# LayerNorm statistics of an out-projection, taken in halves between residual adds in a fixed VectorE order, and a last output tile finished in 128 columns

## The chip, the cores and the metric

One core of one Trainium2 chip. The metric is the device time of one execution in microseconds (us). All runs that are compared here are fast, with a granted TensorE clock of 0.999 or 1.0. A profile's span, from its first to its last instruction, is 1.7 to 2.1 us shorter than the time measured for the same execution. Ratios are the mean time of one kernel's fast runs over that of the other's of the same rounds, so they are not quite the ratio of the medians that are quoted.

## The reference, cut to what matters

Two attention blocks and two token MLPs alternate on `x` of 2048 rows and 1024 columns. The weights are the same both times.

```python
x = x + A(layernorm(x), wqkv, wo)      # local dilated attention, 32 heads, window 8, step 2
x = x + B(layernorm(x), w1, b1, w2, b2)# gelu MLP over the token axis, 3584 hidden
x = x + A(layernorm(x), wqkv, wo)
x = x + B(layernorm(x), w1, b1, w2, b2)
```

The change concerns two places. The first is the end of each `A`: the product with `wo` (the out-projection), the residual add and the statistics of the LayerNorm that follows. The second is the very last tile of the last `B`.

## The kernel before

The out-projection works on 16 tiles of 128 rows. A tile has two halves of 512 columns. Each half takes 8 matmuls into one of two buffers `m` in PSUM (the memory that matmuls write), and then a residual add on VectorE empties the buffer. The first four tiles are interleaved with the last two visits of the attention: a visit makes scores, an exponential on ScalarE, masks on VectorE (`mask`), the products with the values, two passes of a reciprocal on ScalarE, and a normalization on VectorE (`norm`). `chain_` fixes the order of what it wraps on one engine, and `in_order` does so for TensorE; everything else is placed by the scheduler.

```python
psm = pool("psm", 2, space=PSUM)                 # the two m buffers
...
def stats(x, mul, eps):                          # VectorE, then ScalarE
    s = st("bn", [P, NDC, 6])
    for cc in range(NDC):
        nc.vector.bn_stats(out=s[:, cc, :], in_=x[:, cc * 512:(cc + 1) * 512])
    mv = st("mv", [P, 2])
    nc.vector.bn_aggr(out=mv[:], in_=s[:])
    rs = st("rs", [P, 1])
    rsqrt(rs[:], mv[:, 1:2], mul, eps)           # two small ScalarE passes: Ln, Exp
    return mv[:, 0:1], rs
def norm_act(dst, x, mean, rs):
    bi = st("bi", [P, 1])
    nc.vector.tensor_scalar(out=bi[:], in0=mean, scalar1=rs[:], scalar2=-1.0, ...)
    nc.scalar.activation(out=dst, in_=x, func=ACT.Identity, bias=bi[:], scale=rs[:])
...
# out_proj: half(n) = 8 matmuls into an m buffer, add(n) = residual add of it, and
def ln():
    norm_act(h2[c][i][:], xn[:], *stats(xn, 1.0 + EPS, eps2))
...
for vis in range(2 * NU):                        # attention; the last two visits carry tiles 0..3
    ...
    chain_("DVE", mask, 0, 1)                    # (in the last two visits)
    ...
    chain_("DVE", norm.pop())
    for n in range(2):
        half, add, store, ln = out_proj(0, 2 * b + n, ...)
        in_order(half, 0)
        chain_("DVE", add, 0)
        if n == 0:
            chain_("DVE", mask, 2, 3)
        elif lns:
            lns.pop(0)()
        in_order(half, 1)
        chain_("DVE", add, 1)
        store()
        lns.append(ln)
...
for k, (c, i) in enumerate(order[4:]):           # tiles 4..15
    for n in range(2):
        half(n)
        add(n)
    store()
    lns.append(ln)
    for _ in range(2):
        if lns:
            lns.pop(0)()
...
# gemm2, one output tile: 28 matmuls of 512 columns for each half, an add, one store of the tile
for dc in range(NDC):
    for ft in range(FT):
        nc.tensor.matmul(aps[dc], lhsT=w2t[...], rhs=g[...][:, ..., dc * 512:(dc + 1) * 512], ...)
    nc.vector.scalar_tensor_tensor(out=xo[:, dc * 512:(dc + 1) * 512], in0=aps[dc], scalar=b2_sb[...],
                                   in1=xs[:, dc * 512:(dc + 1) * 512], op0=ALU.add, op1=ALU.add)
nc.sync.dma_start(out=dst, in_=xo[:])
```

The softmax here doesn't subtract the row's maximum and nothing guards it: scores larger than these inputs give would overflow.

## Time and profile before

Median 1297.89 us of three runs (1297.88 to 1298.09).

The page's first lines for the kernel before give busy time, share of the span and number of instructions of each engine.

```profile
span 1296.0 us, 19495 instructions
PE 1288.2 (99%) x8414; PEld 591.7 (46%) x8414; DVE 419.3 (32%) x851; ACT 373.4 (29%) x628; POOL 2.4 (0%) x15
```

TensorE (PE) is busy for 99% of the span, so a change to the work of VectorE (DVE) or ScalarE (ACT) can only pay where TensorE waits for it. The list of waits has one entry of the out-projection; its columns are who waited for whom, us in total, times, and the longest.

```profile
PE m L467 <- DVE xn L474: 1.1, 2, 0.6
```

This is the matmul into `m` waiting for the residual add that empties the buffer. The list shows only the two longest of these waits, because a matmul's recorded end lies 0.16 us after the next one could start (379 ns recorded, 216 ns from start to start), and shorter stalls hide inside that. The starts tell more. Measured between weight-load starts, the kernel before has four late matmuls in each out-projection:

| late by, ns | 1st | 2nd | 3rd | 4th | first to last weight load, us |
|---|---|---|---|---|---|
| layer 1 | 188 | 76 | 731 | 101 | 57.587 |
| layer 2 | 190 | 73 | 731 | 97 | 57.580 |

The timeline of layer 1 shows why. Its columns are start, duration, engine, line, operation, output and inputs, count, and in brackets the idle time before it and what ended it. PEld is TensorE's weight load.

```profile
209.28 1.00 DVE L398 TENSOR_TENSOR Pm<-pc,band 32x640 bf16<-32x640 bf16 x2
210.32 0.69 DVE L180 BATCH_NORM_STATS2 bn<-xn 128x6 f32<-128x512 bf16 x1
210.93 0.67 DVE L474 TENSOR_TENSOR xn<-m,xr 128x512 bf16<-128x512 f32 x1
...
211.66 1.39 PEld L467 LDWEIGHTS <-oT 128*128 128x128 bf16 x7 [0.30 <-issue]
...
213.42 1.24 ACT L193 ACTIVATE h<-xn,bi,rs 128x1024 bf16<-128x1024 bf16 x1 [0.28 <-DVE bi L192]
213.47 0.46 PE L383 MATMUL s<-qB,kT 128*32 128x160 bf16 x16
...
214.57 0.78 ACT L386 ACTIVATE pc<-s,shift 128x640 bf16<-128x640 f32 x1
...
216.52 0.69 DVE L437 TENSOR_TENSOR oT<-acc,rd 128x512 bf16<-128x512 f32 x1
217.13 0.68 DVE L474 TENSOR_TENSOR xn<-m,xr 128x512 bf16<-128x512 f32 x1
217.84 0.99 DVE L398 TENSOR_TENSOR Pm<-pc,band 32x640 bf16<-32x640 bf16 x2
217.87 1.60 PEld L467 LDWEIGHTS <-oT 128*128 128x128 bf16 x8 [0.20 <-issue]
218.86 0.21 DVE L192 TENSOR_SCALAR bi<-mv,rs 128x1 f32<-128x1 f32 x1
218.99 0.68 DVE L180 BATCH_NORM_STATS2 bn<-xn 128x6 f32<-128x512 bf16 x1
219.59 0.67 DVE L474 TENSOR_TENSOR xn<-m,xr 128x512 bf16<-128x512 f32 x1
...
220.32 1.89 PE L467 MATMUL m<-wo,oT 128*128 128x512 bf16 x8 [0.57 <-DVE xn L474]
```

The first stall ends at 211.66: the add at 210.93 stood behind half a tile's statistics (L180, 0.69 us). The second ends at 217.87, when the third tile's first add (217.13) has emptied its buffer. The third, the large one, ends at 220.32: the add at 219.59 stood behind two masks (L398), a bias multiply (L192) and another half of statistics (L180). The fourth, of 0.1 us, comes later than the lines shown: the fifth tile's first add (225.57) stood behind the normalization of the last visit. One detail mattered later: on ScalarE the `h` activation of the first tile (L193, 1.24 us) started at 213.42, just ahead of the scores of the next visit at 213.47, and the exponential of these scores (L386) could start only at 214.57.

The tail is the last 512-column add and the store behind it, here in the timeline of the kernel before and then in its list of transfers (size, us from issue to landing).

```profile
1292.24 0.75 DVE L556 SCALAR_TENSOR_TENSOR xo<-m,b_sb,xs 128x512 bf16<-128x512 f32 x1 [5.29 <-PE m L553]
1293.02 0.34 SPq L558 DMA_DIRECT2D out_dram<-xo  x1
```

```profile
out_dram<-xo SPq DMA_DIRECT2D x1, 256.0 KB, 2.0
```

### The profile page before, as it was taken

To read this page: it belongs to the slowest core of one execution; us is meant where nothing else is said; L and a number is where in the kernel's file an instruction comes from. 1 tells how busy PE (TensorE), PEld (TensorE's weight loads), DVE (VectorE), ACT (ScalarE), POOL (GpSimd) and SP (SyncE) were. 2 spreads that over 40 slices of the span, in tenths; PEclk is the share of its full clock that TensorE was granted. 3 is DMA by queue.
4 is the path that set the end of the run, shared out by engine and by line. 5 is a ranking of instruction groups with operands and counts; after the bars stand their busy time and mean duration, and the time that the engine had idled before them with its cause. 6 is when DMAs were issued, how large, how long until landed. Compare 5 with 4: busy or idle time off the path is not lost.

```text
span 1296.0 us, 19495 instructions
## 1 busy us (share of the span) xinstructions
PE 1288.2 (99%) x8414; PEld 591.7 (46%) x8414; DVE 419.3 (32%) x851; ACT 373.4 (29%) x628; POOL 2.4 (0%) x15
## 2 busy tenths in 40 slices
PE   9999999999999999999999999999999999999998
PEld 4444444444444444444444444444444444444443
DVE  7457778810000022322300667688000000111111
ACT  5456665531111110000023666654211111000000
POOL 0000000000000000000000000000000000000000
PEclk9999999999999999999999999999999999999999
DMA  8411123652222235465510111246423222334330
GB/s 235 82 45 47 51 82 115 208 145 82 65 82 75 57 108 140 130 160 135 130 32 1 48 49 50 80 150 211 122 65 91 73 60 84 98 106 140 113 92 33
DMA packets 201574, 125.54 MB, mean 97 GB/s; under 512 B 39824, under 2 KB 183184, under 8 KB 201488
## 3 DMA queue, kind: packets, MB, share of 16 engines
q1 hardware_dynamic: 201488, 124.30, 33.8%
q8 instruction: 66, 1.08, 0.4%
q14 instruction: 20, 0.16, 0.0%
HBM read 96.48 MB, written 16.78 MB: 87 GB/s over the span
## 4 chain that ended last, share of the span: by engine, by line
PE 97%; DVE 1%; ACT 1%; issue 0%; DMA 0%; SPq 0%; DVEq 0%
PE m L352 17%; PE s L553 15%; PE s L510 15%; PE m L553 7%; PE m L510 7%; PE acc L510 7%; PE acc L553 7%; PE m L467 7%; PE m L337 4%; PE m L255 4%; PE s L383 2%; PE acc L418 1%; PE acc L422 1%; DVE xn L474 0%; PE m L268 0%; DVE Pm L398 0%
## 5 line engine op out<-in xcount | busy, mean ns | idle before, releaser
L510 PEld LDWEIGHTS <-w 128*128 128x128 bf16 x1792 | 175.4, 98 | 211.4
L553 PEld LDWEIGHTS <-w 128*128 128x128 bf16 x1792 | 175.3, 98 | 211.5
L352 PE MATMUL m<-hT,wqk 128*128 128x512 bf16 x1024 | 231.7, 380 | 0.0
L510 PE MATMUL s<-h,w 128*128 128x512 bf16 x896 | 202.8, 379 | 0.0
L553 PE MATMUL s<-g,w 128*128 128x512 bf16 x896 | 199.9, 379 | 0.0
L556 DVE SCALAR_TENSOR_TENSOR xo<-s,b_sb,xs 128x512 bf16<-128x512 f32 x32 | 24.0, 751 | 540.7 <-PE s L553 538.6
L352 PEld LDWEIGHTS <-wqk 128*128 128x128 bf16 x1024 | 95.3, 98 | 117.9 <-issue 10.7
L398 DVE TENSOR_TENSOR Pm<-pc,band 32x640 bf16<-32x640 bf16 x256 | 123.6, 483 | 65.8 <-ACT pc L386 56.3
L467 PE MATMUL m<-wo,oT 128*128 128x512 bf16 x512 | 112.5, 379 | 1.2 <-DVE xn L474 1.1
L510 PE MATMUL acc<-h,w 128*128 128x512 bf16 x448 | 103.9, 379 | 0.0
L553 PE MATMUL acc<-g,w 128*128 128x512 bf16 x448 | 100.6, 379 | 0.0
L553 PE MATMUL m<-g,w 128*128 128x512 bf16 x448 | 99.3, 379 | 0.0
L510 PE MATMUL m<-h,w 128*128 128x512 bf16 x448 | 99.0, 379 | 0.0
L174 ACT ACTIVATE ln<-mv,eps 128x1 f32<-128x1 f32 x64 | 18.9, 295 | 233.3 <-DVE mv L182 227.6
L517 ACT ACTIVATE g<-s,b_sb 128x1024 bf16<-128x1024 f32 x28 | 31.2, 1114 | 166.9 <-PE s L510 166.9
L467 PEld LDWEIGHTS <-oT 128*128 128x128 bf16 x512 | 49.5, 98 | 62.6 <-issue 4.5
L363 DVE COPY qB<-qs 32x512 bf16<-32x512 bf16 x136 | 38.1, 280 | 90.4 <-ACT qs L359 89.1
L255 PE MATMUL m<-wv,hT 128*128 128x512 bf16 x256 | 56.1, 379 | 0.7 <-ACT hT L249 0.7
L337 PE MATMUL m<-wv,hT 128*128 128x512 bf16 x256 | 55.4, 379 | 0.0
L359 ACT CAST qs<-m 128x512 bf16<-128x512 f32 x64 | 37.5, 586 | 49.0 <-PE m L352 49.0
L386 ACT ACTIVATE pc<-s,shift 128x640 bf16<-128x640 f32 x64 | 51.2, 799 | 0.3 <-PE s L383 0.3
L356 ACT CAST kT<-m 128x512 bf16<-128x512 f32 x64 | 37.5, 586 | 46.4 <-PE m L352 46.4
(57 smaller groups left out, 674.7 us busy)
## 6 DMA issues: line engine op xcount, KB each, us to landing
w<-in_B_w_dram SPq DMA_DIRECT2D x56, 512.0 KB, 3.8
w<-in_B_w_dram SPq DMA_DIRECT2D x64, 448.0 KB, 4.6
wqk<-in_A_wqkv_dram SPq DMA_DIRECT2D x16, 512.0 KB, 4.8
xa<-xn SPq DMA_DIRECT2D x32, 256.0 KB, 2.3
xs<-xa SPq DMA_DIRECT2D x32, 256.0 KB, 3.2
wv<-in_A_wqkv_dram SPq DMA_DIRECT2D x8, 512.0 KB, 5.5
wo<-in_A_wo_dram SPq DMA_DIRECT2D x8, 512.0 KB, 5.5
xr<-in_A_x_dram SPq DMA_DIRECT2D x16, 256.0 KB, 3.3
```

The source lines that it names most:

```text
L255: r = nc.tensor.matmul(pss_[k, n][:], lhsT=hT[:, kt, cols(*order[k])], rhs=wv[n][kt // 4][:, kt % 4, :], start=(kt == 0), stop=(kt == KD - 1))
L337: nc.tensor.matmul(ps[:], lhsT=hT[:, kt, cols(c, i)], rhs=wv[n][kt // 4][:, kt % 4, :], start=(kt == 0), stop=(kt == KD - 1))
L352: mm = nc.tensor.matmul(ps[:], lhsT=wts[part][:, kt, (g % 2) * P:(g % 2 + 1) * P], rhs=hT[:, kt, lo:lo + 512], start=(kt == 0), stop=(kt = ...
L356: nc.scalar.copy(out=kT[u % 2][:, ls], in_=ps[:])
L359: nc.scalar.copy(out=qs[:], in_=ps[:])
L363: nc.vector.tensor_copy(out=qB[u % 2][hp, h, ls], in_=qs[hp, :])
L386: nc.scalar.activation(out=pc[:].rearrange("p (n t) h k -> p n (t h k)", n=2), in_=ss[:, :, 0:2 * HG * GW], func=ACT.Exp, scale=scale, bia ...
L398: mm = nc.vector.tensor_tensor(out=Pm[rp, :, s0:s0 + HB, r * KG:r * KG + GW].rearrange("p h t k -> p t h k"), in0=pc[rp], in1=mk, op=ALU.mult)
L467: mm = nc.tensor.matmul(ps[:], lhsT=oT[g][:, cols(c, i)], rhs=wo[n][g // 4][:, g % 4, :], start=(g == 0), stop=(g == NG - 1))
L510: nc.tensor.matmul(pairs[fl][0][dc], lhsT=wt[c][:, i, fl * P:(fl + 1) * P], rhs=h2[c][i][:, dc * 512:(dc + 1) * 512], start=(k == 0), stop ...
L517: nc.scalar.activation(out=g[fb][:, fl, :].rearrange("p (n d) -> p n d", n=2), in_=t[:], func=ACT.Gelu_apprx_tanh, bias=b1_sb[:, ft:ft + 1])
L553: nc.tensor.matmul(aps[dc], lhsT=w2t[ft // HF][:, ft % HF, c::DIL], rhs=g[ft // GF][:, ft % GF, dc * 512:(dc + 1) * 512], start=(ft == 0), ...
```

## The change

Its intent: VectorE does at most one half of a tile's statistics between two residual adds, in a fixed order, and computes a tile's bias one step after its statistics, so that it need not wait for ScalarE. The normalization of the last visit moves from ahead of the fifth tile's first add to behind it. The last output tile's second half is computed as 384 and 128 columns and stored in three pieces, so that less work is left after the last matmul.

```diff
-        def ln():
-            norm_act(h2[c][i][:], xn[:], *stats(xn, 1.0 + EPS, eps2))
+        def ln_a():
+            chain_("DVE", stat_half, 0)
+        def ln_b():
+            chain_("DVE", stat_half, 1)
+            chain_("DVE", aggregate)
+            t["rs"] = st("rs", [P, 1])
+            rsqrt(t["rs"][:], t["mv"][:, 1:2], 1.0 + EPS, eps2)
+        def ln_c():
+            chain_("DVE", bias)
+            nc.scalar.activation(out=h2[c][i][:], in_=xn[:], func=ACT.Identity, bias=t["bi"][:], scale=t["rs"][:])
...
+    def ln_step():
+        if late:
+            late.pop()()
+        if lns:
+            parts = lns[0]
+            parts.pop(0)()
+            if len(parts) == 1:
+                late.append(lns.pop(0)[0])
... last two visits:
-                elif lns:
-                    lns.pop(0)()
+                else:
+                    ln_step()
                 in_order(half, 1)
                 chain_("DVE", add, 1)
                 store()
-                lns.append(ln)
+                lns.append(list(ln))
+                if n:
+                    ln_step()
... ahead of tile 4:
-        chain_("DVE", norm.pop())
... tiles 4 to 15:
                 half(n)
-                add(n)
+                chain_("DVE", add, n)
+                ln_step()
+                if norm:
+                    chain_("DVE", norm.pop())
... last tile:
+        parts = [(0, 512, aps[0]), (512, 512, aps[1])]
+        final = not to_hT and (c, i) == order[-1]
+        if final:
+            parts[1:] = [(512, 384, aps[1][:, 0:384]), (896, 128, s_tile()[:, 0, 0:128])]
+        for lo, w, ap in parts:
             ... 28 matmuls of w columns, the add of w columns
+            if final:
+                nc.sync.dma_start(out=dst[:, lo:lo + w], in_=xo[:, lo:lo + w])
+        if not final:
+            nc.sync.dma_start(out=dst, in_=xo[:])
```

More of the change, by code (lines that the diff above doesn't have):

```diff
@@ L478, in store, with stat_half, aggregate, bias @@
             h2[c][i] = vhp.tile([P, D], BF16, name="h2", tag="vh")
-        def ln():
-            norm_act(h2[c][i][:], xn[:], *stats(xn, 1.0 + EPS, eps2))
-        return half, add, store, ln
+        t = {}
+        def stat_half(cc):
+            if cc == 0:
+                t["s"] = st("bn", [P, NDC, 6])
+            return nc.vector.bn_stats(out=t["s"][:, cc, :], in_=xn[:, cc * 512:(cc + 1) * 512])
+        def aggregate():
+            t["mv"] = st("mv", [P, 2])
+            return nc.vector.bn_aggr(out=t["mv"][:], in_=t["s"][:])
+        def bias():
+            t["bi"] = st("bi", [P, 1])
+            return nc.vector.tensor_scalar(out=t["bi"][:], in0=t["mv"][:, 0:1], scalar1=t["rs"][:], scalar2=-1.0, op0=ALU.mult,
+                                           op1=ALU.mult)
+        def ln_a():
[8 more added lines that the diff above has]
+            nc.scalar.activation(out=h2[c][i][:], in_=xn[:], func=ACT.Identity, bias=t["bi"][:], scale=t["rs"][:])
+        return half, add, store, (ln_a, ln_b, ln_c)
+    lns, late = [], []
+    def ln_step():
[6 more added lines that the diff above has]
+                late.append(lns.pop(0)[0])
     pss_ = {}
@@ L550, in gemm2 @@
         aps, _ = pair(i * DIL + c)
-        for dc in range(NDC):
+        parts = [(0, 512, aps[0]), (512, 512, aps[1])]
[3 more added lines that the diff above has]
+        for lo, w, ap in parts:
             for ft in range(FT):
-                nc.tensor.matmul(aps[dc], lhsT=w2t[ft // HF][:, ft % HF, c::DIL],
-                                 rhs=g[ft // GF][:, ft % GF, dc * 512:(dc + 1) * 512],
+                nc.tensor.matmul(ap, lhsT=w2t[ft // HF][:, ft % HF, c::DIL], rhs=g[ft // GF][:, ft % GF, lo:lo + w],
                                  start=(ft == 0), stop=(ft == FT - 1))
-            nc.vector.scalar_tensor_tensor(out=xo[:, dc * 512:(dc + 1) * 512], in0=aps[dc], scalar=b2_sb[:, i, c:c + 1],
-                                           in1=xs[:, dc * 512:(dc + 1) * 512], op0=ALU.add, op1=ALU.add)
-        nc.sync.dma_start(out=dst, in_=xo[:])
+            nc.vector.scalar_tensor_tensor(out=xo[:, lo:lo + w], in0=ap, scalar=b2_sb[:, i, c:c + 1],
+                                           in1=xs[:, lo:lo + w], op0=ALU.add, op1=ALU.add)
+            if final:
+                nc.sync.dma_start(out=dst[:, lo:lo + w], in_=xo[:, lo:lo + w])
+        if not final:
+            nc.sync.dma_start(out=dst, in_=xo[:])
         if to_hT:
@@ L590 @@
             in_order(qk_chunk, 0, wts, part, n)
-        lns = []
         for vis in range(2 * NU):
@@ L639 @@
                 half(n)
-                add(n)
+                chain_("DVE", add, n)
+                ln_step()
+                if norm:
+                    chain_("DVE", norm.pop())
             store()
-            lns.append(ln)
-            for _ in range(2):
-                if lns:
-                    lns.pop(0)()
+            lns.append(list(ln))
+        while lns or late:
+            ln_step()
         g = [None] * NFB
```

## The prediction

> **What bounds the kernel now.** TensorE: on the page 1288.2 us busy of a 1296.0 us span (99%), VectorE 32%; the chain that ended last is 97% TensorE. Only time in which TensorE stands still, or the tail after it, can be won. The matmul starts (216 ns apart where nothing is missing) show gaps of 404, 291, 946 and 317 ns in each layer's out-projection: 188 + 75 + 730 + 101 = 1.09 us too much per layer. The list of waits puts 1.1 us on the residual add (PE m waits for DVE xn). The timeline shows the cause: two m buffers, and a half's add (0.69 us) stands on VectorE behind statistics (0.69), masks (2 x 0.50) and a normalization (0.69). After the last matmul (start 1291.8) come a 512-column add of 0.75 us, a store that lands 2.0 us after its issue at 1293.0, and 0.9 us of closing.
>
> **What the change does.** The comparison of instruction orders shows TensorE unchanged except in the last half tile: 28 matmuls of 512 columns become 28 of 384 and 28 of 128. On VectorE the out-projection's adds come ahead of at most one half of statistics, a tile's statistics run about two tiles later, and its bias waits one step, so that VectorE doesn't wait for ScalarE. SyncE gets two more stores.
>
> **Out-projection, replayed with the trace's durations.** The 188 ns gap goes: the add follows the masks directly. The 75 ns gap grows: ScalarE now puts an `ln` (0.29 us) between the two passes of the reciprocal, so the normalization and the add behind it come 0.1 us later, TensorE 0.19 us earlier: a wait of 0.3 to 0.45 us. The 730 and 101 ns gaps go. Net 0.6 to 0.8 us a layer, 1.4 us in all. After the fourth tile VectorE has about 3.2 us of work per 3.46 us tile: no new gap. The statistics end some 4 us later, but the next stage needs the last tile only 13 us after its start: no cost.
>
> **Tail.** Transposes in this trace, 128 columns with their own weight load, follow each other after 56 ns, so 28 x (162 + 56) = 6.1 us against 6.05: nothing lost. [...] The last add: one element takes 0.21 us, 512 columns 0.75, so about 0.35 for 128: 0.4 less. The last store falls from 256 to 32 KB: its packets (2 KB, 84 ns each) ran for 0.69 us; 256-byte packets elsewhere take 18 ns, so about 0.15: 0.5 less[...]. Two more final semaphores: +0.1. Net -0.8 us.
>
> **Sum:** 1297.9 - 1.4 - 0.8 = 1295.7 us; 8 in 10 between 1294.8 and 1297.0. Faster by over 2%: 0.5%; within 2%: 99%; slower: 0.5%.
>
> **Right if:** the 188 and 730 ns gaps are gone in both layers, one wait of 0.3 to 0.45 us for xn is left; last add near 0.35 us, last store landing near 1.5 us. **Wrong if:** the fixed order makes VectorE wait for ScalarE and so opens new TensorE gaps; [...]the small store lands no sooner.

Of the tail's terms, the 162 ns for 384 columns is an estimate: it lies on the line between the 56 ns for 128 columns and the 216 ns for 512 that the trace of the kernel before shows. So is the +0.1 us for two more final semaphores, in line with the 0.06 us between SyncE's last waits in that trace.

## The result, and the profile after

Median 1295.15 us of six runs (1294.2 to 1296.1), against 1297.93 of six runs of the kernel before (1297.06 to 1298.42). The ratio is 0.998, with a 95% interval of 0.9967 to 0.9992: clear of no change, and within 2%.

The page's first lines of the kernel after, and then, from its list of waits, all that TensorE waited for:

```profile
span 1293.7 us, 19400 instructions
PE 1276.5 (99%) x8286; PEld 593.7 (46%) x8442; DVE 417.3 (32%) x852; ACT 373.2 (29%) x628; POOL 2.4 (0%) x15
```

```profile
PE m L352 <- issue: 4.6, 29, 0.2
PE m L268 <- DVE warm L207: 1.4, 1, 1.4
PE m L255 <- ACT hT L249: 0.7, 1, 0.7
PE s L244 <- DVE x L188: 0.5, 1, 0.5
PE s L383 <- DMA qB<-qs: 0.4, 1, 0.4
PE m L467 <- issue: 0.3, 2, 0.2
```

The wait for `xn` is gone. (This trace has lost 156 matmul records: there are 8442 weight loads and only 8286 matmuls. Gaps of 432 ns between recorded matmuls, one in 50, and the waits put down to "issue" are such losses. The weight loads are complete, so the tables here use their starts.) The timeline of the same stretch of layer 1, which this execution reached 1.3 us later:

```profile
210.59 1.00 DVE L398 TENSOR_TENSOR Pm<-pc,band 32x640 bf16<-32x640 bf16 x2
211.62 0.69 DVE L474 TENSOR_TENSOR xn<-m,xr 128x512 bf16<-128x512 f32 x1
212.97 0.69 DVE L474 TENSOR_TENSOR xn<-m,xr 128x512 bf16<-128x512 f32 x1 [0.66 <-PE m L467]
213.58 0.68 DVE L485 BATCH_NORM_STATS2 bn<-xn 128x6 f32<-128x512 bf16 x1
214.59 0.46 PE L383 MATMUL s<-qB,kT 128*32 128x160 bf16 x16
214.70 0.69 DVE L474 TENSOR_TENSOR xn<-m,xr 128x512 bf16<-128x512 f32 x1 [0.43 <-PE m L467]
215.10 0.80 ACT L386 ACTIVATE pc<-s,shift 128x640 bf16<-128x640 f32 x1 [5.87 <-PE s L383]
...
217.12 0.69 DVE L437 TENSOR_TENSOR oT<-acc,rd 128x512 bf16<-128x512 f32 x1
217.72 0.68 DVE L474 TENSOR_TENSOR xn<-m,xr 128x512 bf16<-128x512 f32 x1
218.44 0.98 DVE L398 TENSOR_TENSOR Pm<-pc,band 32x640 bf16<-32x640 bf16 x2
219.45 0.69 DVE L474 TENSOR_TENSOR xn<-m,xr 128x512 bf16<-128x512 f32 x1
220.84 0.69 DVE L474 TENSOR_TENSOR xn<-m,xr 128x512 bf16<-128x512 f32 x1 [0.69 <-PE m L467]
...
221.68 1.24 ACT L507 ACTIVATE h<-xn,bi,rs 128x1024 bf16<-128x1024 bf16 x1 [4.51 <-DVE bi L493]
```

The second add (211.62) follows the masks directly, the two of 217.72 and 219.45 have only masks between them, and those of 212.97, 214.70 and 220.84 wait for TensorE, not the other way round. The `h` activation of the first tile (now L507) has moved from before the exponential to 221.68. The exponential (L386) starts 0.51 us after the first score (215.10 after 214.59) instead of 1.10 us (214.57 after 213.47).

The tail in the timeline of the kernel after, and, from its list of transfers, the last of the three stores (those of 128 and 96 KB took 1.8 and 1.7 us):

```profile
1289.28 1.73 PE L594 MATMUL s<-g,w 128*128 128x128 bf16 x28
1289.49 0.62 DVE L596 SCALAR_TENSOR_TENSOR xo<-m,b_sb,xs 128x384 bf16<-128x384 f32 x1 [3.80 <-PE m L594]
1291.05 0.35 DVE L596 SCALAR_TENSOR_TENSOR xo<-s,b_sb,xs 128x128 bf16<-128x128 f32 x1 [0.94 <-PE s L594]
```

```profile
out_dram<-xo SPq DMA_DIRECT2D x1, 32.0 KB, 1.4
```

Where the time went, from weight-load starts of the two traces (the end is the start of the last recorded instruction), in us:

| part | before | after | difference |
|---|---|---|---|
| start-up, to the first query product | 65.745 | 66.219 | +0.474 |
| scores, layer 1 | 140.527 | 141.357 | +0.830 |
| out-projection, layer 1 | 57.587 | 56.506 | -1.081 |
| scores, layer 2 | 141.156 | 140.744 | -0.412 |
| out-projection, layer 2 | 57.580 | 56.507 | -1.073 |
| last half tile to the end | 10.159 | 9.136 | -1.023 |
| all of the trace | 1295.942 | 1293.656 | -2.286 |

The rest of the trace agrees to 0.001 us. The three parts that the change touches give -3.18 us together. The other three give +0.89 us, and they vary from run to run whatever the kernel (see the last three experiments).

The tail of 1.02 us splits so: the last add is 0.40 us shorter (0.752 to 0.350). The packets of the last store run 0.242 us from first to last start instead of 0.744. SyncE's wait for the store's semaphore ends 0.39 us after the last packet's start instead of 0.45 (the receipt). From the start of the store's issue to its first packet there are 0.84 us in both. The closing behind it is 0.12 us shorter: SyncE ends with five waits, in the same order before and after; the last store's semaphore was in the third of them, with two more waits of 0.06 us each behind it, and is now in the last. The matmuls take 0.07 us more (6.53 instead of 6.46 us from the half tile's first weight load to the last add).

### The profile page after: what moved, and what is told of

Same layout as the page of the kernel before. It is cut to its first block, busy times and chain, and to the rows that moved or that the text cites. A ratio compares the mean times of both kernels' runs of the same rounds, so it can differ in the third digit from the quotient of the medians.

```text
span 1293.7 us, 19400 instructions
## 1 busy us (share of the span) xinstructions
PE 1276.5 (99%) x8286; PEld 593.7 (46%) x8442; DVE 417.3 (32%) x852; ACT 373.2 (29%) x628; POOL 2.4 (0%) x15
## 3 DMA queue, kind: packets, MB, share of 16 engines
q8 instruction: 66, 1.08, 0.3%
## 4 chain that ended last, share of the span: by engine, by line
PE 98%; issue 1%; DVE 0%; DMA 0%; ACT 0%; SPq 0%
PE m L352 17%; PE s L594 15%; PE s L547 15%; PE m L467 8%; PE acc L547 7%; PE m L547 7%; PE acc L594 7%; PE m L594 7%; PE m L337 4%; PE m L255 4%; PE s L383 2%; PE acc L418 1%; PE acc L422 1%; PE m L268 0%; DMA qB<-qs 0%
## 5 line engine op out<-in xcount | busy, mean ns | idle before, releaser
L352 PE MATMUL m<-hT,wqk 128*128 128x512 bf16 x963 | 223.3, 379 | 6.2 <-issue 4.6
L594 PE MATMUL s<-g,w 128*128 128x512 bf16 (+1 forms) x912 | 201.0, 374 | 0.7
L596 DVE SCALAR_TENSOR_TENSOR xo<-s,b_sb,xs 128x512 bf16<-128x512 f32 (+1 forms) x33 | 24.4, 739 | 532.9 <-PE s L594 527.6
L594 PE MATMUL m<-g,w 128*128 128x512 bf16 (+1 forms) x436 | 96.9, 376 | 0.6
L386 ACT ACTIVATE pc<-s,shift 128x640 bf16<-128x640 f32 x64 | 51.2, 800 | 12.2 <-PE s L383 12.1
```

The costliest lines, as they stand in the source:

```text
L352: mm = nc.tensor.matmul(ps[:], lhsT=wts[part][:, kt, (g % 2) * P:(g % 2 + 1) * P], rhs=hT[:, kt, lo:lo + 512], start=(kt == 0), stop=(kt = ...
L386: nc.scalar.activation(out=pc[:].rearrange("p (n t) h k -> p n (t h k)", n=2), in_=ss[:, :, 0:2 * HG * GW], func=ACT.Exp, scale=scale, bia ...
L594: nc.tensor.matmul(ap, lhsT=w2t[ft // HF][:, ft % HF, c::DIL], rhs=g[ft // GF][:, ft % GF, lo:lo + w], start=(ft == 0), stop=(ft == FT - 1))
```

## The experiments

All gave correct results. Their times scatter by 0.5 us and more around the median, as large as the effects asked about. The verdicts on mechanism therefore rest on the traces: the out-projection's length from first to last weight load (56.506 to 56.508 us in every trace without a stall) and the length of the tail.

| run | median, us | before, same rounds | ratio [95%] | out-projection, layers 1 and 2, us | tail, us |
|---|---|---|---|---|---|
| changed kernel | 1295.15 | 1297.93 | 0.998 [0.9967, 0.9992] | 56.506, 56.507 | 9.136 |
| e1_order_only | 1296.08 | 1298.27 | 0.9986 [0.9973, 0.9998] | 56.508, 56.506 | 10.161 |
| e2_tail_only | 1297.42 | 1298.27 | 0.9992 [0.998, 1.0005] | 57.582, 57.578 | 9.152 |
| e3_free_order | 1297.28 | 1298.27 | 0.9993 [0.998, 1.0005] | 57.574, 57.584 | 9.138 |
| e4_no_late | 1296.36 | 1298.27 | 0.9986 [0.9972, 1.0] | 57.284, 57.284 | 9.136 |
| e5_early_h | 1295.88 | 1297.99 | 0.9985 [0.997, 1.0] | 56.644, 56.644 | 9.138 |
| e6_late_h | 1296.97 | 1297.99 | 0.9993 [0.9976, 1.001] | 57.246, 57.244 | 9.140 |
| e7_one_store | 1295.65 | 1297.99 | 0.9985 [0.997, 1.0] | 56.507, 56.507 | 9.833 |
| e8_half256 | 1295.11 | 1297.99 | 0.9978 [0.9963, 0.9993] | 56.506, 56.508 | 9.405 |
| e9_unsplit | 1294.7 | 1297.83 | 0.9975 [0.9962, 0.9989] | 56.507, 56.506 | 9.135 |
| e10_load_b1 | 1295.4 | 1297.83 | 0.9978 [0.9964, 0.9991] | 56.505, 56.505 | 9.147 |
| e11_after_again | 1295.74 | 1297.83 | 0.9983 [0.997, 0.9995] | 56.507, 56.507 | 9.130 |
| e12_qb_vec | 1295.19 | 1298.04 | 0.9977 [0.9964, 0.9991] | 56.506, 56.508 | 9.144 |

### The two parts alone

e1: the changed kernel without its tail.

```diff
-        final = not to_hT and (c, i) == order[-1]
+        final = False
```

> The change without its tail part: the out-projection order of the changed kernel, the last tile stored whole as before. If the two parts simply add, the four gaps of TensorE in each layer's out-projection (1.09 and 1.05 us too much, by the weight-load starts of before) are gone here and the time after the last matmul is as before: about 2.1 us less than before, 1295.8. The recorded reasoning (a wait of 0.3 to 0.45 us left in each layer) would give only 1.4 us less, 1296.5.

e2: the kernel before, with only the new last tile.

> The kernel before with only the 384 + 128 column tail. Gaps of the out-projection as before (1.09 and 1.05 us); from the last matmul's start to the end of the span about 1.0 us less than before (last add 0.35 instead of 0.75 us, store packets 0.24 instead of 0.74 us, receipt slightly sooner), so about 1296.9. Rival: [...]the gain is only the 0.4 us of the add, 1297.5.

The out-projection of e1 is as short as that of the changed kernel and its tail as long as before; in e2 it is the reverse. In the traces the parts simply add: 2.15 us and 1.01 us. So e2's rival, a gain of the add's 0.4 us alone, is out. The timed means say 1.83 us (e1) and 1.00 us (e2) less, but their intervals are over 3 us wide. The reasoning, which left a wait of 0.3 to 0.45 us in each layer, is refuted by e1: there is none.

### Is it the fixed order, or the splitting?

e3: the changed kernel, with the pieces split as there but not fixed on VectorE.

```diff
         def ln_a():
-            chain_("DVE", stat_half, 0)
+            stat_half(0)
... the same for stat_half 1, aggregate, bias, and for add in tiles 4 to 15
```

> The changed kernel with the same split statistics, but VectorE's order left to the scheduler again (only the first four tiles' adds, masks and normalizations are fixed, as before). The built order on VectorE is nearly that of before. If the fixed order does it, all four gaps come back (about 1.05 us a layer), and the gain shrinks to the tail's 1.0 us: 1296.9. Rival: splitting the statistics and holding back the bias does it, whatever the order: no gaps, 1294.8.

The four late matmuls came back, within 5 ns of those before (186, 71, 728, 97 ns late in layer 1), and the list of waits shows the old entry again:

```profile
PE m L467 <- DVE xn L474: 1.1, 2, 0.6
```

The scheduler had put the statistics back where they were before. The split pieces are worth nothing without the fixed order.

e9: the opposite, a fixed order without the split. Both halves of the statistics stand together and only the aggregation is separate.

```diff
         def ln_a():
             chain_("DVE", stat_half, 0)
+            chain_("DVE", stat_half, 1)
         def ln_b():
-            chain_("DVE", stat_half, 1)
             chain_("DVE", aggregate)
```

> The changed kernel with both halves of a tile's statistics in one piece (1.28 us on VectorE) at the first step and only the aggregation at the second; order otherwise fixed as there. If one half at a time between two adds is what keeps TensorE fed, an add now comes up to 0.7 us later and gaps for xn appear in the out-projection (some 0.1 to 0.5 us a layer, since a half of matmuls lasts 1.73 us). If only keeping the statistics off the first visits matters, the out-projection lasts 56.51 us from first to last weight load, as in the changed kernel.

There was no gap: 56.507 and 56.506 us. So "one half between two adds" is not what pays. What pays is that the adds come first in the crowded visits and the statistics wait until VectorE has room for them; a piece of 1.28 us still fits behind an add while TensorE spends 1.73 us on the next half. The median of 1294.7 us is the lowest of all, but its runs (1294.02 to 1295.6) overlap with those of the changed kernel.

### What the bias's delay does

e4: the bias and the `h` activation follow their statistics at once.

```diff
             if len(parts) == 1:
-                late.append(lns.pop(0)[0])
+                lns.pop(0)[0]()
```

> The changed kernel with the bias multiply and the h activation right behind a tile's statistics instead of one step later. The bias multiply then stands on VectorE ahead of the masks of the last visit but one and waits for ScalarE (rs comes behind the exponential and the two reciprocal passes): the normalization and the add behind it come about 1.3 us later than in the changed kernel, so TensorE waits about 0.8 us once in each layer: 1.6 us more than the changed kernel, 1296.7. Rival: holding back makes no difference, 1295.1.

TensorE waited 0.78 us once in each layer (57.284 against 56.507), as expected. The timeline of e4 shows the chain:

```profile
216.12 0.21 DVE L493 TENSOR_SCALAR bi<-mv,rs 128x1 f32<-128x1 f32 x1 [0.98 <-ACT rs L175]
216.25 0.96 DVE L398 TENSOR_TENSOR Pm<-pc,band 32x640 bf16<-32x640 bf16 x2
217.25 0.69 DVE L437 TENSOR_TENSOR oT<-acc,rd 128x512 bf16<-128x512 f32 x1
217.86 0.68 DVE L474 TENSOR_TENSOR xn<-m,xr 128x512 bf16<-128x512 f32 x1
...
218.59 3.62 PE L467 MATMUL m<-wo,oT 128*128 128x512 bf16 x16 [0.60 <-DVE xn L474]
```

VectorE stands idle 0.98 us for `rs`, which ScalarE makes behind the exponential. The masks, the normalization and the add wait behind it, and TensorE waits for the add. That the change holds the bias back by one step is thus worth 1.56 us over the two layers.

### Why the second gap went too

The prediction expected the 75 ns gap to grow. It vanished. The trace offers two theories. Theory V says that VectorE's order alone does it. Theory S says that ScalarE has a part in it: with the statistics late, the first tile's `h` activation (1.24 us) no longer stands ahead of the exponential on which masks, normalization and the third tile's add depend. e5 and e6 change one side at a time.

e5: the fixed order is kept, but the first tile's statistics and `h` are done early, so that `h` is again ahead of the exponential. (The whole of these statistics now stands ahead of the second tile's first add, which runs 0.70 us later than in the changed kernel. So not all adds come ahead of the statistics, as the text below has it; no matmul was late for that one.)

```diff
+                early = b == 0 and n == 1
+                if early:
+                    first_ln = lns.pop(0)
+                    first_ln[0]()
+                    first_ln[1]()
                 chain_("DVE", add, 0)
                 if n == 0:
                     chain_("DVE", mask, 2, 3)
+                elif early:
+                    first_ln[2]()
                 else:
                     ln_step()
... and no ln_step() at the end of that tile
```

> The changed kernel, but the first tile's statistics, bias and h activation are done one tile earlier, so that its h activation (1.24 us) stands on ScalarE ahead of the exponential of the next visit, as it did before; on VectorE the adds still come ahead of the statistics. Theory V (VectorE's order alone closes the gaps): no gaps, as in the changed kernel. Theory S (part of the gain is that the h activation no longer holds up the exponential, hence masks, normalization and the third tile's add): one gap of 0.3 to 0.4 us for xn comes back in each layer, at the start of the fourth tile's matmuls; the others stay gone. In time 0.7 us more than the changed kernel.

One gap came back, at the start of the fourth tile's matmuls, where theory S puts it. It is 128 ns in layer 1 and 129 in layer 2 (0.14 us with what follows), not 0.3 to 0.4. In the timeline of e5 the exponential waits for `h`:

```profile
214.53 0.46 PE L383 MATMUL s<-qB,kT 128*32 128x160 bf16 x16
214.53 1.24 ACT L507 ACTIVATE h<-xn,bi,rs 128x1024 bf16<-128x1024 bf16 x1 [0.28 <-DVE bi L493]
...
215.68 0.78 ACT L386 ACTIVATE pc<-s,shift 128x640 bf16<-128x640 f32 x1
...
216.49 0.97 DVE L398 TENSOR_TENSOR Pm<-pc,band 32x640 bf16<-32x640 bf16 x2 [1.16 <-ACT pc L386]
...
217.63 0.69 DVE L437 TENSOR_TENSOR oT<-acc,rd 128x512 bf16<-128x512 f32 x1 [0.17 <-ACT rd L435]
218.24 0.68 DVE L474 TENSOR_TENSOR xn<-m,xr 128x512 bf16<-128x512 f32 x1
```

It starts 1.15 us after the first score (215.68 after 214.53), against 0.51 us in the changed kernel. VectorE stands idle 1.16 us for it before the masks, so it is ScalarE that makes the add late here, and not what VectorE had to do.

e6: the reverse. VectorE's order is free (in the built program it is the same as that of e3 through this stretch), but `h` is forced behind the reciprocal's second pass on ScalarE.

```diff
... VectorE's order free, as in e3
+            with tc.issue_after(last["RD"].ins):     # last["RD"]: the reciprocal's second pass
                 nc.scalar.activation(out=h2[c][i][:], in_=xn[:], func=ACT.Identity, bias=t["bi"][:], scale=t["rs"][:])
```

> The counterpart: VectorE's order left to the scheduler (nearly as before), but the h activations are forced behind the reciprocal's second pass on ScalarE. Theory V: all gaps as before (about 1.05 us a layer). Theory S: the first gap (0.19 us) stays, the 75 ns gap goes, and the large one shrinks from 0.73 to about 0.5 us, since the masks and the add ahead of it come about 0.3 us earlier: 0.75 us a layer left.

Two late matmuls are left, 192 and 555 ns in layer 1 (190 and 556 in layer 2), 0.74 us a layer, against 1.07 of e3. The 75 ns gap and the 100 ns gap are gone and the large one has shrunk by 0.17 us, with VectorE's order left as it was. In the timeline of e6 the exponential is early again, 0.51 us after the first score; the first tile's `h` runs at 216.61.

```profile
214.25 0.46 PE L383 MATMUL s<-qB,kT 128*32 128x160 bf16 x16
...
214.76 0.80 ACT L386 ACTIVATE pc<-s,shift 128x640 bf16<-128x640 f32 x1 [0.85 <-PE s L383]
```

This is theory S. That its sum (0.75 us left) was met is in part chance: the large gap kept 0.555 us instead of 0.5, and the fourth, which the text does not speak of, went (ScalarE no longer puts the second tile's `h` ahead of the last visit's reciprocal). So ScalarE's side alone removes 0.33 us a layer, VectorE's side alone (e5) 0.94 of 1.08 us, and both together all of it; the two overlap.

### The tail

e7: matmuls and adds as in the changed kernel, but one store of the whole tile after the last add.

```diff
-            if final:
-                nc.sync.dma_start(out=dst[:, lo:lo + w], in_=xo[:, lo:lo + w])
+            if final and lo == 896:
+                nc.sync.dma_start(out=dst, in_=xo[:])
```

> The changed kernel, with the last tile's matmuls and adds split as there, but its 256 KB stored in one piece after the last add. The add's part of the tail gain (0.4 us) stays, the store's part (0.55 us: packets run 0.74 us again) goes: from the last add's end to the end of the span as before (3.0 us). Rival: the store's size does not matter and the span ends as in the changed kernel.

The tail took 9.833 us, 0.70 us more than in the changed kernel and 0.33 less than before. From the add's end to the last recorded instruction it is 2.95 us again, as before (2.95), against 2.26. So the short add is worth 0.33 us net (0.40 less the matmuls' 0.07) and storing in three pieces 0.70 us, more than the 0.55 expected: 0.50 for the packets, 0.07 for the receipt, and 0.12 for the closing. This last part is not the store's size. In e7 its semaphore is in the third of SyncE's five waits again, as in the other two traces with one store of the last tile (before and e1), and two waits follow; in all traces with three stores it is in the last.

e8: two pieces of 256 columns.

```diff
-            parts[1:] = [(512, 384, aps[1][:, 0:384]), (896, 128, s_tile()[:, 0, 0:128])]
+            parts[1:] = [(512, 256, aps[1][:, 0:256]), (768, 256, s_tile()[:, 0, 0:256])]
```

> The last half tile as 256 + 256 columns instead of 384 + 128: rows of 512 bytes in the last store. Last add about 0.48 us (worked out from 0.35 for 128 and 0.75 for 512 columns), store packets about 0.3 us: 0.2 us more than the changed kernel after the last matmul. [...]

The tail took 9.405 us, 0.27 more than with 128 columns. The add took 0.485 us, and the packets of 512 bytes ran for 0.316 us (0.242 with 256 bytes). That accounts for 0.21 of the 0.27; the receipt took the rest (0.44 against 0.39 us). A packet took 26 ns with 512 bytes, and 18 ns with 256. The packets of 256 bytes thus ran for 0.07 us less and their receipt came 0.05 us sooner: no cost of the smaller rows is seen here. In time the kernels with 128 and 256 columns cannot be told apart (1295.15 and 1295.11).

### Why the parts that were not touched vary

In the score stages TensorE sometimes waits within a visit's scores for a small transfer, the copy of two query heads (`qB<-qs`), and these stages differ by up to 1.0 us between traces. Two experiments (e10 and e12) looked for the cause, to see whether a better kernel lies there.

e10: the load of the next query and key weights goes behind the copies of its unit.

```diff
-            if b == 0 and u % (2 * DIL) == 1 and u + 3 < NU:
+            if b == 1 and u % (2 * DIL) == 1 and u + 3 < NU:
```

> Not about the change itself: the changed kernel, with each load of the next query and key weights (two of 512 KB) issued half a visit pair later, behind the small copies of that pair's queries instead of shortly before the next ones. In the traces so far TensorE waits now and then for such a copy in the middle of a visit's scores, 0.2 to 0.6 us at a time, at the visits that follow the weight load, before and after the change alike. If the weight load holds them up, these waits go and the two score stages last 140.5 us each: 0.3 to 1.0 us less than the changed kernel in the mean. If the copies are late for another reason, it runs as the changed kernel.

e11: the changed kernel again.

> The changed kernel itself once more, on the same chip as the two others: 1295.1 us, out-projection 56.51 us in both layers, and the tail as in its first profile; the score stages and the start-up are expected to differ from the first profile by some tenths of a microsecond.

The waits within scores added up to 1.51 us in e10 and 1.78 us in e11, in single profiles (0.84 in the kernel before, 1.30 in the changed kernel's first profile). Moving the weight load did not take them away. They account for what differs between the score stages: without these waits both stages together last 280.8 to 281.0 us in every trace but e12's. In e11 the out-projection was as in the first profile, to 0.001 us.

e12: for six of the query units VectorE does the copies that were transfers.

```diff
-                if h < HG // 2 or u == 0:
+                if h < HG // 2 or u in (0, 5, 6, 7, 9, 10, 13):
```

> Not about the change itself, but about the spread between its runs: the changed kernel, with the query copies of head 2 and 3 of each group (32 x 512, 0.28 us each) done by VectorE instead of by a transfer, for the six query units whose scores waited in the traces so far. In those traces every wait within a visit's scores comes 0.6 to 2.5 us after the start of a 16 KB packet of the instruction queue that takes 0.9 to 1.4 us, with the last packet of a query copy ending late, and issuing the weight loads elsewhere did not take the waits away. If the copy transfers behind such a packet are the cause, the waits go, both score stages last about 140.5 us and the time is 0.7 to 1.3 us below the changed kernel, 1294.3. If VectorE's 1.1 us more per unit delays the masks or normalizations, other waits of up to 0.3 us per unit appear and eat the gain. If the waits have another cause, they stay.

The waits at these six units' scores were gone, in one profile; each of the other 13 traces has at least one there. A unit left as it was waited 0.70 us, with a 16 KB packet of the instruction queue (1.52 us long) starting 1.9 us before its scores. Twelve new waits of 0.13 to 0.30 us appeared at the products with the values, as they would if VectorE's longer work delayed the masks, and nothing was gained: 1295.19 us. So these waits are for the copies made as transfers: where VectorE makes the copy there is none. That an instruction packet delays the transfer is not tested by itself: at every wait of over 0.06 us in the six traces looked through (before, after, e9 to e12) such a packet had started within 4.5 us before the scores, but most visits that had such a packet lost nothing (26 of 30 in the changed kernel's first profile). No version beat the changed kernel clearly.

## Why the prediction was right

The predicted time was 1295.7 us, and 1295.15 was measured, inside the range of 1294.8 to 1297.0. The median fell by 2.8 us, where the prediction said 2.2. That the time lay inside the range is in part luck: with only the parts that the change touches, 3.18 us less in the traces, it would have been 1294.75, just below it. Both parts of the sum were predicted too small, and start-up and score stages, which the change does not touch, hid some of that.

- **What bounds the kernel** was right: only TensorE's stalls and the tail could be won, and no other part changed by design.
- **The 188, 730 and 101 ns gaps** went, as predicted, and e3 shows that the fixed order removed them.
- **"The 75 ns gap grows ... a wait of 0.3 to 0.45 us" was wrong.** The replay counted two delays: an `ln` between the two passes of the reciprocal, and TensorE 0.19 us earlier. The `ln` did come there and cost 0.05 us (the passes start 0.67 us apart instead of 0.62). What the replay overlooked is that the statistics' new place also moved the `h` activation, which had held the exponential up. The exponential now starts 0.51 us after the first score instead of 1.10, and the third tile's first add 3.13 us after it instead of 3.66, in time. So the out-projection gave 1.08 us a layer, not 0.7: 2.15 us in all against 1.4. e6 confirms the mechanism. With the activation in the way again (e5), it and the add came 0.05 us later after the first score than in the kernel before, and the wait was longer by as much, 128 ns instead of 75; no `ln` stood between the passes there, so the replay's two delays are not tested by it.
- **The tail**: -0.8 us predicted, -1.02 measured. The add (0.350 us for 0.35), the packets (0.5 us less) and the matmuls (those of 384 columns 162 to 163 ns apart, those of 128 columns 55 to 56) were right. (The half tile's matmuls took 0.07 us more in all, where the prediction counted no loss.) "Two more final semaphores: +0.1" was wrong: SyncE ends with five waits as before, and the last store's semaphore came to be in the last of them, which made the closing 0.12 us shorter. Nobody had aimed at that. The receipt, 0.07 us sooner, was not foreseen either.
- **The median moved less than the traced parts.** -3.18 us in the parts touched stand against 2.8 us in the first rounds and 2.1 us in e11's (medians 1297.83 and 1295.74). The single profiles put the rest into the start-up and the score stages, which vary by such amounts. That the change makes them longer does not show: start-up and score stages together last 347.4 us in the profile of the kernel before and 347.0 in e2's, which is the kernel before up to its last half tile, and 346.7 to 349.0 us in the eight profiles with the changed order and these stages untouched (the changed kernel, e1, e4, e5, e7, e8, e9, e11). With two profiles on one side a few tenths stay open.

## What to carry to other kernels

When an engine feeds a nearly saturated TensorE through two buffers, put the instruction that frees a buffer first in program order and let everything that nobody waits for fall behind; fixing that order mattered here (without it the out-projection of layer 1 took 57.574 us instead of 56.506, e3), and cutting the work into pieces did not (56.507 us with both halves of the statistics together, e9). When instructions are moved on one engine, follow what they trigger on the others: here a 1.24 us activation left the path of an exponential, which the prediction had missed. After the last matmul, the size of the last store and of the last add were both on the path here (0.50 us less of packets for 32 instead of 256 KB, 0.40 us less for an add of 128 instead of 512 columns), so finish with a narrow piece, as long as its matmuls with their weight loads do not slow down (here 0.07 us).
